# Front end and tail of a one-core H3 convolution and MLP kernel: k at the head of its queue, identity products on TensorE, a gate behind its copy, and a new written-out order

## The chip, the cores and the metric

The kernel runs on one core of one Trainium2 chip. The metric is the device time of one execution in microseconds (us). It was run three times before the change; the median is 254.28 us. Five engines work side by side: PE (TensorE, matrix products), DVE (VectorE), ACT (ScalarE), POOL (GpSimd) and SP, which only issues transfers. Products land in PSUM and must be copied ("evacuated") to SBUF by ACT or DVE.

## The reference, cut to what matters

```python
def _A_ref(q, k, v, shift_k, ssm_k, ssm_D):        # B, S, D = 1, 2048, 512; 4 shift taps
    k_shift = sum over t of  k_pad[:, t:t+S, :] * shift_k[:, 3-t]
    kv = k_shift * v
    y = irfft(rfft(kv, 2S) * rfft(ssm_k, 2S))[:S] + kv * ssm_D     # a long causal convolution
    return q * y
def _B_ref(x, w1, b1, w2, b2):                     # F = 1376
    return gelu(layernorm(x) @ w1 + b1) @ w2 + b2

x = A_q
x = x + _A_ref(layernorm(x), A_k, A_v, A_shift_k, A_ssm_k, A_ssm_D)
x = x + _B_ref(layernorm(x), B_w1, B_b1, B_w2, B_b2)
x = x + _A_ref(layernorm(x), ...)                  # the same k, v and filters again
x = x + _B_ref(layernorm(x), ...)
return x
```

The convolution's result y does not depend on x, so it is computed once and used twice.

## The kernel before, in words

There are two stages. The first, up to about 110 us, computes y by a transform written as matrix products, and starts on the first MLP. Its work is cut into pieces that are added to a `_Plan`; the order of the pieces, the engine that does each and the buffers that each takes stand in one long string, `ORDER`, written out by hand or by a search outside the kernel. `plan.write` emits the pieces in that order, so each engine works through its own pieces strictly in the order of the string. A word such as `kT3.P2` says: piece kT3, on PE, PSUM buffer 2 (there are four, of 1024 f32 each); `kT3e.A` says that its evacuation is done by ACT (D for DVE, G for POOL, S for a transfer issued by SP).

The pieces, in the order in which the data flow (lines of the kernel before):

- `lSK`, `lk0` to `lk3`, `lv0`, `lv1`, `lx0`, `lh…`, `lK..`: loads of the shift weights' row (into `SKr`, L164), of k (four transfers of 512 KB), v, the first group of x, edge rows of k, and the long filter (issued at L279 and L352). All stand on SP's one queue.
- `Dz` (L193): POOL spreads ssm_D, which a transfer from ACT's queue puts at byte 80 K of one large tile, the arena.
- `bS`, `bSK` (L364, L415): the shift weights turned into columns and broadcast by products with one row; `dg0` to `dg2` (L423) build diagonal matrices from them.
- `kT0` to `kT3` (L431): PE transposes of a quarter of k each, 12 per piece; evacuated at L217 (DVE) or L215 (ACT).
- `kv..` (L513): the shifted k as 32 products with the diagonals per piece; `kvm` (L519) multiplies with v on DVE. For the fourth column block POOL does the same by itself (`kg`, `ka`, `kgm`, L445 to L456). `s00` is the first layer norm's statistics.
- `U.S.` (L303), `KS` (L390), `U.T.` (L335, or by DMA transposes for the last column block, L282): first transform stage of kv and of the filter. `K2` (L403): second stage of the filter. `sa`, `sb`: eight SBUF to SBUF transfers of its result.
- `X` (L543), `T` (L558, DVE), `V` (L567): second stage of kv, product with the filter, first inverse stage; per column block 4 of each.
- `Z` (DMA transposes, L614) and `TC`, `TD` (PE transposes, L602); `Y` (L634): last inverse stage; `Y..e` copies Y into SBUF.
- per unit of rows of the first group, 0, 1 and 2 to 3: the gate `g0` (L660, L661: times normalised x, added to x), statistics `h0` (L237 to L243), POOL's power `p0` (L249), normalisation `b0` (L254), transposes `LT` (L642), and the first MLP product with GELU, `M` (L689, L697).

The second stage is a loop over eight groups of rows with products L726 (w1) and L760 (w2).

The gate reads the PSUM buffer of Y00 or Y01 itself, where `Y00e` and `Y01e` read the same buffer to copy it. The order before puts g00 ahead of Y00e, and Y01e ahead of g01.

Of the kernel before, what the change touches and what calls it, by code (L numbers as in the profile page):

```python
# [104 lines left out]
def kernel(ctx: ExitStack, tc: tile.TileContext, A_q, A_k, A_v, A_shift_k, A_ssm_k, A_ssm_D,  # L105
                 B_x, B_w1, B_b1, B_w2, B_b2, out):
    nc = tc.nc
    P = 128
    _, S, D = A_q.shape
    F = B_w1.shape[1]  # L110
    KS = A_shift_k.shape[1]
# [101 lines left out]
    def evac(eng, dst, src):  # L213
        if eng == "A":
            nc.scalar.activation(dst, src, AF.Copy)  # L215
        else:
            nc.vector.tensor_copy(dst, src)  # L217
# [56 lines left out]
    with tc.tile_pool(name="ps", bufs=1, space=bass.MemoryType.PSUM) as ps:  # L274
# [3 lines left out]
        def load(name, dst, src, nbytes, deps=(), eng="S", rank=0):  # L278
            return plan.add(name, {eng: 400}, deps, lambda it: nc.sync.dma_start(dst, src), dma=("copy", nbytes), rank=rank)  # L279
# [147 lines left out]
        for q in range(4):  # L427
            def mms(o, q=q):
                for i in range(4):
                    for ct in range(CK):  # L430
                        nc.tensor.transpose(o[:, i, ct, :], kn[:, 4 * q + i, ct * P:ct * P + P], IDt[:])  # L431
# [214 lines left out]
        for n, (a, b) in enumerate(UNITS):  # L646
            xs, ln, m = x_t[:, a:b, :], lna0[:, a:b, :], b - a
            if m == 1:
                y = plan.add(f"Y0{a}", {"P": 432}, e0[n] + [lH], lambda it, a=a: last_mm(0, a, 1)(
                    view(pf[it["slot"]["ps"]], [1, D])), take=["ps"])  # L650
                yf = [(y, "ps")]
                plan.add(f"Y0{a}e", {"A": 520, "D": 600}, [y], lambda it, y=y, a=a: evac(
                    it["eng"], YA[0][:, a:a + 1, :], view(pf[y["slot"]["ps"]], [1, D])), free=yf, rank=1)
            else:
                _, y = mm_evac("Y02", 864, e0[1] + [lH], last_mm(0, 2), [2, D], lambda: YA[0][:, 2:4, :])
                yf = []

            def gate(it, m=m, y=y, xs=xs, ln=ln, a=a, b=b):
                ya = YA[0][:, a:b, :] if m == 2 else view(pf[y["slot"]["ps"]], [1, D])
                nc.vector.tensor_tensor(ln, ln, ya, ALU.mult)  # L660
# [180 lines left out]
```

## Time and profile before

| | us |
|---|---|
| three runs | 257.37, 254.15, 254.28 |
| median | 254.28 |
| the profiled execution | 257.37 |
| its span, first to last instruction | 255.7 |
| granted TensorE clock, mean | 0.991 |
| PE, DVE, ACT, POOL busy | 237.9, 168.9, 145.6, 54.6 |
| first `kv` product starts | 15.57 |
| first product of `M` starts | 93.79 |
| loop's first product (L760) starts | 109.58 |

The profile shows one execution. "The chain of waits" follows the end of the program back to its start: each row has a start, a length and what was done there. "The timeline" lists the instructions of one engine; what stands in square brackets is the idle time before and what ended it. "The table by windows" gives busy time of each engine in a stretch of time, the number of instructions, the granted clock, and the DMA engines' share and rate.

### The profile page before, as it was taken

To read this page: it belongs to the slowest core of one execution; us is meant where nothing else is said; L and a number is where in the kernel's file an instruction comes from. 1 tells how busy PE (TensorE), PEld (TensorE's weight loads), DVE (VectorE), ACT (ScalarE), POOL (GpSimd) and SP (SyncE) were. 2 spreads that over 40 slices of the span, in tenths; PEclk is the share of its full clock that TensorE was granted. 3 is DMA by queue.
4 is the path that set the end of the run, shared out by engine and by line. 5 is a ranking of instruction groups with operands and counts; after the bars stand their busy time and mean duration, and the time that the engine had idled before them with its cause. 6 is when DMAs were issued, how large, how long until landed. Compare 5 with 4: busy or idle time off the path is not lost.

```text
span 255.7 us, 4760 instructions
## 1 busy us (share of the span) xinstructions
PE 237.9 (93%) x1907; PEld 150.5 (59%) x1919; DVE 168.9 (66%) x312; ACT 145.6 (57%) x221; POOL 54.6 (21%) x50
## 2 busy tenths in 40 slices
PE   1599999999999959999999999999999999999994
PEld 1489887799898748844444444444444444444443
DVE  0137789879999875787889899876866862022022
ACT  3677789999999667951722712812812812713700
POOL 4089999700000030111111101110110110000000
PEclk9999999999999988999999999999999999999999
DMA  2999997593959894013040402104006006001001
GB/s 72 313 309 226 198 363 299 242 387 123 288 119 159 212 243 160 3 23 62 0 85 0 82 0 55 30 0 82 1 22 146 0 21 146 1 26 57 3 33 49
DMA packets 51104, 29.65 MB, mean 116 GB/s; under 512 B 44707, under 2 KB 48520, under 8 KB 49802
## 3 DMA queue, kind: packets, MB, share of 16 engines
q1 hardware_dynamic: 50930, 29.21, 42.9%
q8 instruction: 15, 0.25, 0.4%
q10 hardware_dynamic: 152, 0.14, 0.2%
q14 instruction: 7, 0.06, 0.1%
HBM read 16.23 MB, written 2.10 MB: 72 GB/s over the span
## 4 chain that ended last, share of the span: by engine, by line
PE 78%; DMA 8%; ACT 5%; DVE 5%; issue 1%; SPq 1%; POOL 0%; ACTq 0%
PE po L760 30%; PE ph L726 26%; PE p L689 5%; PE p L513 4%; DMA arena<-ZT 4%; ACT arena L215 4%; DMA arena<-in_A_k_dram 3%; PE p L335 2%; PE p L543 2%; PE p L403 2%; ACT ZT L215 2%; PE p L303 1%; PE p L567 1%; PE p L634 1%; PE p L602 1%
## 5 line engine op out<-in xcount | busy, mean ns | idle before, releaser
L728 ACT ACTIVATE arena<-ph,B 128x512 bf16<-128x512 f32 (+1 forms) x77 | 52.7, 687 | 78.9 <-PE ph L726 78.9
L760 PE MATMUL po<-arena 128*128 128x512 bf16 (+3 forms) x355 | 77.0, 372 | 0.4
L726 PE MATMUL ph<-arena 128*128 128x512 bf16 (+1 forms) x308 | 67.6, 379 | 0.0
L760 PEld LDWEIGHTS <-arena 128*128 128x128 bf16 (+1 forms) x363 | 35.4, 98 | 40.7
L726 PEld LDWEIGHTS <-arena 128*128 128x128 bf16 (+1 forms) x308 | 30.8, 100 | 35.9
L765 DVE TENSOR_TENSOR arena<-po,arena 128x512 bf16<-128x512 f32 (+1 forms) x33 | 21.5, 672 | 44.3 <-PE po L760 44.3
L215 ACT ACTIVATE arena<-p 128x1024 bf16<-128x1024 f32 (+7 forms) x41 | 38.2, 1020 | 8.1 <-DVE arena L660 2.1
L249 POOL TENSOR_TENSOR lrsm<-lrsm,mhalf 128x4 f32<-128x4 f32 (+2 forms) x10 | 9.3, 926 | 94.0 <-DVE lrsm L243 94.0
L217 DVE COPY arena<-p 128x2048 bf16<-128x2048 bf16 (+4 forms) x13 | 12.9, 996 | 20.0 <-PE p L431 13.3
L215 ACT ACTIVATE ZT<-p 128x1024 bf16<-128x1024 f32 (+1 forms) x23 | 22.7, 1025 | 2.9 <-PE p L303 2.9
L237 DVE BATCH_NORM_STATS2 lstm<-arena 128x6 f32<-128x512 bf16 x32 | 20.0, 681 | 0.2
L558 DVE TENSOR_TENSOR T<-xb,arena 128x2048 bf16<-128x2048 bf16 (+1 forms) x17 | 18.9, 1152 | 0.0
L249 POOL TENSOR_TENSOR lrsg<-lrsg,mhalf 128x4 f32<-128x4 f32 x8 | 8.1, 1010 | 47.5 <-DVE lrsg L246 47.5
L237 DVE BATCH_NORM_STATS2 lstg<-arena 128x6 f32<-128x512 bf16 x28 | 17.2, 679 | 0.0
L445 POOL TENSOR_TENSOR T<-arena,SK 128x2048 bf16<-128x2048 bf16 (+3 forms) x4 | 14.9, 3744 | 9.3 <-ACT arena L215 9.1
L567 PE MATMUL p<-arena,T 128*128 128x128 bf16 x256 | 16.2, 219 | 0.8 <-ACT ZT L215 0.6
L254 DVE TENSOR_SCALAR arena<-arena,lmvg,lrsg 128x512 bf16<-128x512 bf16 x32 | 11.1, 409 | 7.9 <-POOL lrsg L249 7.9
L567 PEld LDWEIGHTS <-T 128*128 128x128 bf16 x256 | 15.0, 98 | 1.4 <-issue 0.8
L217 DVE CAST arena<-p 128x1024 bf16<-128x1024 f32 x13 | 15.3, 1219 | 0.7 <-PE p L390 0.6
L215 ACT ACTIVATE xb<-p 128x1024 bf16<-128x1024 f32 x14 | 14.4, 1048 | 0.1
L689 PE MATMUL p<-arena 128*128 128x128 bf16 (+3 forms) x132 | 11.8, 260 | 2.3 <-ACT arena L215 2.3
L513 PE MATMUL p<-DG,arena 128*128 128x128 bf16 x192 | 13.2, 235 | 0.0
(78 smaller groups left out, 250.4 us busy)
## 6 DMA issues: line engine op xcount, KB each, us to landing
arena<-arena SPq DMA_DIRECT2D x8, 512.0 KB, 5.3
arena<-in_A_k_dram SPq DMA_DIRECT2D x4, 512.0 KB, 6.2
arena<-in_A_v_dram SPq DMA_DIRECT2D x2, 1024.0 KB, 9.5
arena<-in_A_ssm_k_dram SPq DMA_DIRECT2D x4, 512.0 KB, 10.2
arena<-tabM SPq DMA_DIRECT2D x1, 2048.0 KB, 10.4
out_dram<-arena SPq DMA_DIRECT2D x15, 128.0 KB, 1.7
arena<-in_A_q_dram SPq DMA_DIRECT2D x1, 1536.0 KB, 7.7
arena<-in_B_w_dram SPq DMA_DIRECT2D x1, 1376.0 KB, 7.1
```

The costliest lines, as they stand in the source:

```text
L215: nc.scalar.activation(dst, src, AF.Copy)
L217: nc.vector.tensor_copy(dst, src)
L237: nc.vector.bn_stats(self.st[:, i, 0, :], x_t[:, GT * g + i, :] if src is None else src[:, i, :])
L249: nc.gpsimd.tensor_tensor(self.rs[:, a:b], self.rs[:, a:b], mhalf[:, a:b], ALU.pow)
L513: nc.tensor.matmul(o[:, i, :], w, DG[:, cc, t, :], start=t == 0, stop=t == KS - 1)
L558: eng.tensor_tensor(view(Tb[it["slot"]["T"]], [2, n, CW]), x2, kk, ALU.mult)
L567: nc.tensor.matmul(o[:, i, :], T[:, r, i, :], Mt[:, ka + i, 1 - r, :], start=r == 0, stop=r == 1)
L689: nc.tensor.matmul(o[0:m, ft - f0, :].rearrange("p (i t) -> p i t", t=P), W1t[:, ct, ft * P:ft * P + m], lnT[0][:, a:b, ct, :], start=ct = ...
L726: nc.tensor.matmul(o.rearrange("p (i t) -> p i t", t=P), W1t[:, ct, ft * P:ft * P + m], lt[:, a:b, ct, :], start=ct == 0, stop=ct == CT - 1)
L728: nc.scalar.activation(hT[0:m, ft, a * P:b * P], o, AF.Gelu_apprx_tanh, bias=B1[0:m, ft:ft + 1])
L760: nc.tensor.matmul(po[:, a:b], hT[0:m, ft, i * P:(i + 1) * P], W2t[0:m, ft, a:b], start=ft == 0, stop=ft == FT - 1)
L765: nc.vector.tensor_tensor(xs, po[:, a:b], xs, ALU.add)
```

## The change

Five edits, of which the last moves nearly every piece of the first stage:

1. `SKr`, the shift weights' row, moves from byte 80 K to 81 K of the arena, off the bytes into which ssm_D is loaded; `junk`, a scratch output of `s00`, moves from 84 K to 80 K.
2. k comes in two transfers of 1 MB instead of four of 512 KB (`lk1`: quarters 2 and 3, `lk0`: quarters 0 and 1).
3. Three new pieces `wm0` to `wm2`: 32, 4 and 4 products of the identity with itself, whose output nobody reads.
4. The gate of units 0 and 1 depends on the copy `Y0.e`, so that a written order must put the copy first.
5. A new `ORDER`.

```diff
-    SKr = at(80 * K, [[1, D * KS]], 0, 1)
+    SKr = at(81 * K, [[1, D * KS]], 0, 1)
...
-    junk = place("junk", [P, D], 84 * K)
+    junk = place("junk", [P, D], 80 * K)
...
-        lk = [load(f"lk{q}", kn[:, 4 * q:4 * q + 4, :], kd4[:, 4 * q:4 * q + 4, :], 2 ** 19) for q in range(4)]
+        lk = [load(f"lk{q}", kn[:, 8 * q:8 * q + 8, :], kd4[:, 8 * q:8 * q + 8, :], 2 ** 20) for q in range(2)]
...
+        def warm(it):
+            o = view(pf[it["slot"]["ps"]], [8, P])
+            for i in range(it["n"]):
+                nc.tensor.matmul(o[:, i % 8, :], IDt[:], IDt[:], start=True, stop=True)
+        for i, n in enumerate((32, 4, 4)):
+            it = plan.add(f"wm{i}", {"P": 107 * n}, [], warm, take=["ps"])
+            it["n"] = n
+            it["free"] = [(it, "ps")]
...
-                plan.add(f"Y0{a}e", {"A": 520, "D": 600}, [y], lambda it, y=y, a=a: evac(
+                ye = plan.add(f"Y0{a}e", {"A": 520, "D": 600}, [y], lambda it, y=y, a=a: evac(
...
-            ga = plan.add(f"g0{a}", {"D": 1190 if m == 2 else 930}, [y, s2, lx], gate, free=yf)
+            ga = plan.add(f"g0{a}", {"D": 1190 if m == 2 else 930}, [y, ye, s2, lx], gate, free=yf)
...
-lSK.S bSK.P0 bSKe.A bS.P2 lk3.S lk1.S lk0.S lk2.S lh113.S bSe.A ...
+lk1.S wm1.P0 wm0.P1 lSK.S wm2.P0 bS.P0 bSe.D dg1.D lk0.S dg0.A lh113.S bSK.P1 bSKe.A ...
```

What it moves, at three places. First SP's queue at the start of the program (k is `in_A_k_dram`, the shift weights' row `in_A_shift_k_dram`, the long filter `in_A_ssm_k_dram`); before:

```order
L279 DMA arena<-in_A_shift_k_dram 1x2048 [waits DMAHW1_49,Pool_49]
L279 DMA arena<-in_A_k_dram 128x2048 x4
L279 DMA kh<-in_A_k_dram 15x3x128
L279 DMA kh<-in_A_k_dram 112x3x128 [waits DMAHW0_49]
L279 DMA arena<-in_B_b_dram 1x1376
L279 DMA arena<-in_A_q_dram 128x2048 [waits DMAHW2_49]
L279 DMA arena<-in_A_v_dram 128x4096 [waits DMAHW3_49]
L352 DMA arena<-in_A_ssm_k_dram 128x32x64 [waits DMAHW4_49]
```

and after the change:

```order
L279 DMA arena<-in_A_k_dram 128x4096
L279 DMA arena<-in_A_shift_k_dram 1x2048
L279 DMA arena<-in_A_k_dram 128x4096
L279 DMA kh<-in_A_k_dram 15x3x128
L279 DMA kh<-in_A_k_dram 112x3x128
L279 DMA arena<-in_B_b_dram 1x1376
L279 DMA arena<-in_A_q_dram 128x2048 [waits DMAHW0_49]
L279 DMA arena<-in_A_v_dram 128x4096 [waits DMAHW1_49]
```

The first load of the queue no longer waits for POOL and for the load of ssm_D, k stands ahead of the shift weights, and both loads of v stand ahead of the long filter.

Second, DVE from the last inverse stage to the start of the MLP (L660 and L661 are the gate, L669 and L670 after the change; `lstm`, `lmvm`, `lrsm` are the statistics of a unit); before:

```order
L660 TENSOR_TENSOR arena<-arena,p_120 128x512
L661 TENSOR_TENSOR arena<-arena 128x512
L237 BN_STATS lstm_108<-arena 128x6
L241 BN_AGGR lmvm_109<-lstm_108 128x2
L243 TENSOR_SCALAR lrsm_110<-lmvm_109 128x1
L660 TENSOR_TENSOR arena<-arena 128x1024
L661 TENSOR_TENSOR arena<-arena 128x1024
L254 TENSOR_SCALAR arena<-arena,lmvm_109,lrsm_110 128x512
L237 BN_STATS lstm_108<-arena 128x6 x2
```

and after the change, where row 0's unit comes first and its copy out of PSUM (`L217 CAST`) is DVE's own:

```order
L217 CAST arena<-p_117 128x512
L669 TENSOR_TENSOR arena<-arena,p_117 128x512
L670 TENSOR_TENSOR arena<-arena 128x512
L237 BN_STATS lstm_108<-arena 128x6
L241 BN_AGGR lmvm_109<-lstm_108 128x2
L243 TENSOR_SCALAR lrsm_110<-lmvm_109 128x1
L669 TENSOR_TENSOR arena<-arena,p_120 128x512
L670 TENSOR_TENSOR arena<-arena 128x512
L254 TENSOR_SCALAR arena<-arena,lmvm_109,lrsm_110 128x512
```

The units now run in the order 0, 1, 2 to 3 (before: 1, 2 to 3, 0), and the gate of a two-row unit no longer stands between the first unit's statistics and its normalisation.

Third, ACT at the same place; before (the row that waits for DVE alone is the copy Y00e, and the 512-wide row behind it LT1e):

```order
L215 ACTIVATE arena<-p_118 128x1024 [waits DVE_49,PE_49]
L215 ACTIVATE arena<-p_119 128x512 [waits DVE_49]
L215 ACTIVATE arena<-p_117 128x512 [waits PE_49]
L215 ACTIVATE arena<-p_120 128x8x256
L215 ACTIVATE arena<-p_118 128x1024 [waits PE_49]
```

and after the change (the first 512-wide row is Y01e, the second LT0e):

```order
L215 ACTIVATE arena<-p_120 128x512 [waits PE_49]
L215 ACTIVATE arena<-p_119 128x1024
L215 ACTIVATE arena<-p_118 128x8x256 [waits PE_49]
L215 ACTIVATE arena<-p_120 128x512 [waits DVE_49,PE_49]
L215 ACTIVATE arena<-p_119 128x1024
```

Y00e has left ACT; the copy of the first transposed unit, LT0e, waits for DVE only because the PSUM buffer that its transposes took was read by the gate g01.

More of the change, by code (lines that the diff above doesn't have):

```diff
@@ L18 @@
 ORDER = """
-lSK.S bSK.P0 bSKe.A bS.P2 lk3.S lk1.S lk0.S lk2.S lh113.S bSe.A dg2.A dg0.A dg1.A lh1.S kg0.G kT3.P2 kT1.P0 kT1e.A kT3e.D kT0.P1 lb1.S kT0e.D kT2.P2 lx0.S lv0.S bB.P0 lK00.S lK01.S lv1.S kT2e.D kv20.P1 bBe.D lK11.S lK10.S kv00.P0 s00.A kvm20.D U2S0.P20 kvm00.D kv10.P1 U2S0e.D U2S1.P0 U2S1e.A U0S0.P31 U0S1.P2 kvm10.D U1S0.P12 U1S0e.D kv01.P0 U0S1e.A U0S0e.A kg1.G kd0.P1 U1S1.P2 kvm01.D kv11.P3 kvm11.D s01.G U1S1e.A kd0e.A KS11.P2 KS11e.A KS01.P1 KS01e.A KS30.P0 U0S2.P3 U0S2e.A KS30e.D KS00.P2 KS20.P1 KS21.P0 KS00e.D KS10.P3 KS20e.A KS10e.D kv21.P2 kd4.P3 KS21e.A U1S2.P0 kvm21.D kd4e.A U1S2e.A KS31.P1 KS31e.A lH.S KS51.P3 KS61.P2 KS51e.D KS61e.A KS41.P0 KS41e.D KS71.P1 KS50.P3 KS60.P2 KS71e.A KS50e.D KS40.P0 KS60e.A KS70.P1 lX.S KS70e.A KS40e.D U1S3.P3 U2S3.P2 U2S3e.D lW.S K22.P0 U1S3e.A K20.P1 K20e.D K23.P3 K25.P2 K22e.A K23e.A K25e.D K212.P0 K26.P1 K212e.A K21.P3 K26e.A lM.S K215.P2 K21e.D K210.P0 K27.P1 K210e.D K215e.A sa0.S K27e.A K29.P3 K24.P2 K24e.A U2S2.P0 K213.P1 K213e.A K29e.D sb0.S ka1.G kg2.G ka2.G kg3.G ka3.G K28.P3 K28e.A U2S2e.D U1T0.P2 K211.P0 sb1.S sa1.S K211e.A K214.P1 K214e.A U1T0e.D U2T0.P3 U0S3.P0 sa2.S sb3.S kgm.G U0S3e.A X10.P20 U2T0e.D U1T1.P1 X10e.A U1T1e.D X21.P31 U3S0.P02 U2T1.P2 U3S1.P1 X21e.A T10.D0 U3S0e.A U3S1e.A X20.P32 U0T0.P0 U2T1e.D X20e.A sb2.S sa3.S U3S3.P1 U3S3e.A X12.P20 T21.D1 X12e.A U0T0e.D U0T1.P3 X11.P11 U3S2.P0 T20.D2 U0T1e.D V10.P21 X11e.A U3S2e.A lx.S V10e.A U3T0.S ly.S U3T1.S V20.P10 X22.P32 T11.D0 T12.D2 X22e.A V21.P0 T22.D1 V21e.A X23.P21 X23e.A V20e.A X01.P30 V11.P0 V11e.A X01e.D V12.P2 X00.P32 X00e.A T23.D0 T01.D2 V22.P1 X13.P01 V12e.A T00.D1 X13e.A X03.P30 V23.P2 X03e.A V00.P0 V22e.D X02.P12 V23e.A T13.D0 T03.D1 V01.P3 X30.P21 X02e.A T02.D2 V01e.D V00e.A X30e.A V13.P1 V13e.A Z10.S Z11.S T30.D0 V03.P0 X32.P22 X31.P30 X31e.D X32e.A V03e.A V02.P1 T32.D2 V02e.A T31.D1 X33.P21 X33e.A TC0a.P0 V30.P32 V30e.A V32.P1 T33a.D0 V31.P2 T33b.D2 V33a.P3 TC0ae.D V32e.A V33ae.D Z03.S V33b.P1 TC0b.P0 Z00.S V31e.A V33be.A TD0a.P3 s02.D TC0be.A TD0ae.A TD0b.P2 TC1.P1 Z01.S TD0be.D Y01.P3 Y01e.A TC1e.D Y02.P2 g01.D h01.D TC3.P0 Y02e.A g02.D p01.G Y10.P1 TC3e.A w4.S b01.D Y00.P2 Y10e.A h02.D g00.D TC2.P3 Y00e.A w1.S LT1.P0 p02.G b02.D LT1e.A Y12.P1 h00.D TC2e.A M1a.P0 M1b.P2 LT2.P3 w3.S Z12.S Z13.S p00.G Z02.S Y12e.A M1be.A LT2e.D Y32.P1 M1ae.A M2a.P2 Y32e.A b00.D LT0.P3 M2b.P0 LT0e.A M2ae.A M2be.A M0a.P3 M2c.P2 M0ae.A M0b.P0 M0be.A M2ce.A Y20.P1 Y20e.A LG1.D Y22.P3 Y22e.A w2.S Y30.P0 Y30e.A
@@ new lines @@
+lk1.S wm1.P0 wm0.P1 lSK.S wm2.P0 bS.P0 bSe.D dg1.D lk0.S dg0.A lh113.S bSK.P1 bSKe.A lh1.S dg2.D kT3.P2 kT2.P0 kT2e.D kT3e.A lb1.S lx0.S lv0.S kT0.P1 lv1.S kT1.P3 kT0e.A bB.P2 bBe.A kT1e.D kv00.P1 kvm00.D kv10.P3 U0S0.P10 kv01.P2 kvm10.D U1S0.P31 s00.A U0S0e.A kvm01.D kv20.P0 U1S0e.D U0S3.P2 U0S1.P1 kv21.P3 U0S3e.D lK01.S U0S1e.A kvm20.D kvm21.D lK00.S kd0.P1 U1S1.P2 U2S0.P02 kd0e.A KS20.P1 U1S1e.A KS20e.D U2S0e.A KS21.P3 KS21e.A KS11.P2 lK11.S lK10.S KS11e.D lH.S KS00.P0 KS00e.D lX.S KS01.P1 KS31.P3 KS31e.A KS01e.A kv11.P2 KS30.P3 kd4.P0 KS10.P1 kd4e.A kvm11.D KS10e.D lW.S KS30e.A KS40.P0 kg0.G KS60.P2 KS60e.D KS61.P3 KS40e.A KS41.P1 KS71.P0 KS61e.A KS41e.D KS70.P2 KS71e.A KS70e.A KS50.P3 KS50e.D KS51.P1 U0S2.P0 U1S2.P2 U0S2e.D U2S3.P3 KS51e.A K210.P1 K211.P0 K210e.D U1S2e.A U2S3e.A kg1.G K29.P2 K29e.A K211e.D K214.P3 K23.P1 K214e.A K27.P2 K23e.D K20.P0 K22.P3 K20e.D K27e.A lM.S U1S3.P1 K22e.A s01.G K21.P2 K21e.D K25.P0 K213.P3 K213e.D U1S3e.A K25e.A K215.P1 K215e.A sa0.S K28.P2 K26.P0 ka1.G kg2.G ka2.G kg3.G K26e.D ka3.G K212.P3 U1T0.P1 K212e.D K24.P0 K28e.A sb0.S U0T0.P2 U2S2.P3 K24e.A U2S2e.A U1T0e.D U1T1.P0 U0T0e.D X10.P10 U1T1e.D X00.P31 U2S1.P2 X10e.A kgm.G U2S1e.A X00e.D U3S0.P01 sa3.S U3S0e.A T10.D0 U3S3.P1 X01.P22 U0T1.P3 X01e.A sa1.S U3S1.P0 X13.P20 sb1.S T00.D1 sb3.S U3S3e.A U2T0.P1 U0T1e.D U3S1e.A X13e.A U3S2.P3 sb2.S U3S2e.A V00.P0 V00e.A T01.D2 V10.P20 U2T0e.D X20.P12 T13.D1 X02.P31 V10e.A sa2.S X02e.A V13.P0 lx.S X20e.D T20.D0 X12.P20 V01.P1 V13e.A X12e.A X03.P32 V01e.A X03e.A T02.D1 U2T1.P0 T12.D2 X11.P21 U2T1e.D V20.P12 V12.P3 T03.D0 X11e.A V20e.A T11.D2 V12e.A X21.P00 X23.P22 X23e.D X21e.A V02.P1 X22.P31 V03.P0 T21.D1 U3T0.S V02e.A X22e.A T23.D0 V11.P2 X30.P10 ly.S U3T1.S V03e.A X30e.A V21.P3 X32.P02 T22.D2 X31.P11 V11e.A T30.D1 X31e.D X32e.A V23.P2 T32.D0 V21e.A V23e.A V30.P01 Z00.S Z01.S X33.P10 X33e.A Z10.S V22.P3 V22e.A V30e.A T31.D1 V32.P2 Z11.S Z03.S T33a.D2 T33b.D0 V32e.D V31.P1 V33a.P3 V33b.P0 TC0b.P2 w3.S w1.S V33ae.D V31e.A TC0a.P1 V33be.A TC0ae.D s02.D TC0be.A TD0a.P0 TD0b.P3 TD0ae.A w4.S TC1.P1 Y00.P0 TD0be.A Y02.P2 TC1e.A Y00e.D g00.D h00.D Y01.P3 Y01e.A g01.D p00.G Y02e.A TC2.P1 TC2e.A b00.D TC3.P0 Y12.P2 h01.D p01.G LT0.P3 g02.D LT0e.A Y12e.A Y10.P1 Y10e.A M0a.P3 b01.D LT1.P2 Z02.S Z12.S Z13.S LT1e.A h02.D M0b.P1 M0ae.A TC3e.D M1a.P2 M0be.A M1b.P0 p02.G b02.D LT2.P3 M1be.A LT2e.A Y30.P1 Y22.P0 M2b.P3 Y30e.A M1ae.A M2be.A M2a.P1 M2ae.A w2.S M2c.P2 M2ce.A Y32.P3 Y32e.A Y22e.A Y20.P1 Y20e.A LG1.D
```

5 lines of the change are left out of this document (3 added, 2 removed).

## The prediction

> **What bounds the kernel now.** I read the page first, for the span, and then the chain of waits, because its rows say what each stretch waits for.
>
> ```profile
> span 255.7 us, 4760 instructions
> ```
>
> ```profile
> 0.80 0.35 ACTq L184
> ...
> 3.37 0.25 POOL Dz L193
> ...
> 3.63 0.35 SPq L279
> ...
> 5.41 8.28 DMA arena<-in_A_k_dram
> ...
> 13.73 1.46 PE p L431 x12
> 15.19 0.38 PE p L370 x11
> 15.57 5.35 PE p L513 x64
> ...
> 25.10 1.79 PE p L513 x32
> ...
> 82.61 0.60 ACT ZT L215
> ...
> 93.79 4.24 PE p L689 x44
> ...
> 109.58 8.43 PE po L760 x39
> ```
>
> Read from the top: ACT issues its first transfer at 0.80, but SP's queue stands until POOL has spread ssm_D (3.37 to 3.62), because the shift weights' row overwrites those bytes. So k's last quarter lands at 13.69, and TensorE's real work, the kv products, starts at 15.57. From 109.58 to the end the chain is TensorE without a gap, in a loop that the change leaves as it is: the 146.1 us from there to 255.7 stay. Everything is decided by how much earlier L760 starts. Between the two, the table by windows shows which engine is full:
>
> ```profile
> core 0: us, PE busy (x) PEld busy (x) DVE busy (x) ACT busy (x) POOL busy (x), PEclk, DMA share, GB/s
> 42.00:53.00 11.00, 10.88 (x167) 9.00 (x162) 9.22 (x9) 10.58 (x13) 7.44 (x2) 1.00 0.59 241
> 53.00:65.00 12.00, 11.83 (x189) 11.54 (x186) 11.32 (x11) 12.00 (x14) 0.00 (x0) 1.00 0.71 247
> 65.00:75.50 10.50, 9.95 (x169) 9.61 (x169) 10.50 (x10) 10.50 (x13) 0.00 (x0) 1.00 0.85 226
> ```
>
> PE is full from 42 to 53, ACT from 53 on, DVE with it from 65. There is no stall to take out of this stretch; it can only start earlier or hold fewer pieces. Two slow spells of TensorE stand in the same table (columns as above):
>
> ```profile
> 12.20:15.60 3.40, 3.18 (x38) 2.71 (x36) 1.33 (x2) 1.88 (x2) 1.75 (x1) 1.00 1.07 402
> 15.60:19.00 3.40, 3.40 (x34) 3.40 (x35) 0.66 (x2) 3.24 (x10) 3.40 (x2) 1.00 1.16 239
> 19.00:22.40 3.40, 3.40 (x59) 3.35 (x58) 2.69 (x3) 2.69 (x8) 3.32 (x3) 1.00 1.04 165
> 90.70:94.10 3.40, 1.13 (x13) 0.71 (x11) 3.33 (x10) 1.45 (x3) 0.70 (x1) 1.00 1.23 227
> 94.10:97.50 3.40, 3.40 (x36) 3.40 (x34) 0.56 (x3) 2.32 (x2) 1.07 (x2) 0.50 0.95 263
> ```
>
> From 94.1 to 97.5 the granted clock is 0.50, after a window in which PE worked a third of the time. The column reads 1.00 at the start, yet kv is slow there: 64 products took 5.35, while 32 later ones took 1.79, 56 ns each. With twice 56 ns for the slow ones, 32 of the 64 were slow, 3.6 us. The rows agree: 34 products in 15.60 to 19.00, 59 in the next 3.40.
>
> **The change part by part.** *The head of SP's queue.* With the row moved, the first load (now k) can go when SP is free, about 0.80 as on ACT, where k's first load started at 4.05: 3.25 earlier.
>
> ```profile
> arena<-in_A_k_dram SPq DMA_DIRECT2D x1, 512.0 KB, 4.1
> 10.75 2.76 PE L431 MATMUL p<-IDt,arena 128*128 128x128 bf16 x24 [1.09 <-DMA arena<-in_A_k_dram]
> 15.23 0.96 DVE L217 COPY arena<-p 128x1536 bf16<-128x1536 bf16 x1 [0.72 <-PE p L431]
> ```
>
> *k in two loads.* Four loads took 13.69 - 4.05 = 9.64 from first issue to last landing (the first alone 4.1). No row shows a 1 MB load of k. Below: 2.1 MB at the 402 GB/s of the row 12.20 to 15.60 is 5.2; the first load's 4.1 less 1.3 at that rate leaves 2.8 of start-up, so landing 8.8. Above: as before plus ACT's tables in the way, 11.7. Same bytes, same queue, so I take 9.6, landing at 10.4. But now a half is transposed behind the last landing, not a quarter: 24 transposes of 2.76 (before 1.46), and kT1's copy of 0.96 on DVE stands ahead of the first kv. 10.4 + 2.76 + 0.96 + 0.2 of handing over is 14.3 against 15.57: **-1.3**. Had k stayed in quarters, the same landing would have given -3.2.
>
> *Identity products.* The forty have their operand at about 2.0 and nothing else to do; at 56 to 112 ns they take 2.2 to 4.5, over by 6.5, before half of k can have landed. They cost nothing; if k came early they would delay transposes that wait for the second half anyway, by at most 0.5. What they bring is bounded by the slow spells: 32 kv products at 56 ns less, 1.8, and about 1.0 of the 2.76 above. I take 0: between them and kv lie some 7 us in which PE does transposes and waits, and row 12.20 to 15.60 shows that transposes filling 3.18 of 3.40 did not speed it up.
>
> [...]
>
> *The middle.* The new order moves pieces but adds no work.
>
> ```profile
> 41.33 0.27 PE L403 MATMUL p<-arena,Wt 64*128 64x256 bf16 x1 [0.19 <-ACT arena L215]
> 52.62 0.61 PE L543 MATMUL p<-arena,Wt 128*128 128x128 bf16 x8
> 53.74 2.02 ACT L215 ACTIVATE xb<-p 128x1024 bf16<-128x1024 f32 x2
> 41.98 8.48 ACT L215 ACTIVATE arena<-p 128x1024 bf16<-128x1024 f32 x9
> 71.38 3.48 DVE L558 TENSOR_TENSOR T<-xb,arena 128x2048 bf16<-128x2048 bf16 x3
> ```
>
> Until the first K2 (41.33) PE now has one U product piece fewer (0.44): 41.33 - 1.3 - 0.4 = 39.6. From there to the first X (52.62, 11.3 later) one more piece of transposes (1.0): 51.9. From the first X's copy on, ACT has 31 copies of 1024 in both orders; at 8.48 / 9 = 0.93 with the last instruction's tail off they take 28.8, and before they ran 53.74 to 82.6 without a gap. Now the first X's copy can start at 52.5, as its two predecessors on ACT are done. That ends at 81.3, and V33be, the half copy behind them (82.61, 0.60), at 82.0 where it was 83.2: **-1.2**. DVE has 22 pieces of 1.13 from its first product T on, 25 us of the 27 to there: hidden under ACT. Bounds: 0, if U3T1 (below) lands when it did, to -2.0, if PE's piece fewer counts in full.
>
> *The tail.* The chain from V33be to the first M product took 93.79 - 83.2 = 10.6.
>
> ```profile
> 86.48 0.69 DVE L660 TENSOR_TENSOR arena<-arena,p 128x512 bf16<-128x512 bf16 x1 [0.17 <-ACT arena L215]
> 87.66 0.69 DVE L237 BATCH_NORM_STATS2 lstm<-arena 128x6 f32<-128x512 bf16 x1
> 88.68 0.68 DVE L660 TENSOR_TENSOR arena<-arena 128x1024 bf16<-128x1024 bf16 x1
> 88.84 0.96 POOL L249 TENSOR_TENSOR lrsm<-lrsm,mhalf 128x1 f32<-128x1 f32 x1 [39.32 <-DVE lrsm L243]
> 90.01 0.41 DVE L254 TENSOR_SCALAR arena<-arena,lmvm,lrsm 128x512 bf16<-128x512 bf16 x1
> 92.65 3.77 ACT L215 ACTIVATE arena<-p 128x512 bf16<-128x512 f32 x4 [2.13 <-DVE arena L660]
> ```
>
> The last row is the copy Y00e: ACT stood 2.13 for the gate g00 on DVE, with LT1e, which M waits for, queued behind. Now: TD0a, TD0b and TC1 on PE 1.7, Y00 0.45, its copy on DVE 0.7, gate 1.15 (86.48 to 87.66), statistics 1.05 (to 88.68). While POOL takes the power (0.96), DVE does unit 1's gate, 1.15; then normalisation 0.4, LT0 0.3, its copy 0.55, handing over 0.4: 7.8. The first M starts at 89.8: **-2.8** more. Y01's gate now waits for ACT's copy, done while DVE is at unit 0. Bounds: -4 (TC1 not in the way) to 0 (a late DMA transpose Z, or w1, decides).
>
> *M.* 132 products and the Y's between them took 109.58 - 93.79 = 15.8, of which 44 took 4.24 for 2.46 at 56 ns: 1.8 of slow clock. PE now has Y12, LT0 and Y10 (2.0 in all) in the 2.3 before the first M, so the slow spell is less likely; I keep 0.5 of 1.8: **-1.3**, bounds -1.8 to 0.
>
> *Sum.* -1.2 (start and middle), -2.8, -1.3: -5.3. [...] I add 0.6 for that: **-4.7**. The profiled span would be 251.0. The profiled execution took 257.37, 3.1 above the median, 1.7 of it outside the span; I carry the difference over to the median: 254.28 - 4.7 = **249.6**.
>
> **The rivals.** *A: the clock stays fast into kv.* For it: forty products and an earlier kv. Against: row 12.20 to 15.60. It gives 1.8 and some of the 1.0 more, 2.4: 247.2.
>
> *B: the middle gives the start back.* The fourth column block goes through two DMA transposes in a queue behind eight copies and a load of x.
>
> ```profile
> 64.85 0.54 SPq L279
> ...
> 65.44 9.98 DMA arena<-ZT
> ...
> 75.47 1.19 PE p L543 x16
> ```
>
> Landing at 75.42, it held X32 up by a moment. My walk has its input 2.2 earlier, but sa and sb now wait for K2 pieces further apart. If it lands when it did, the 1.2 is lost, and with 0.6 of the tail's bounds used: 251.4.
>
> [...]
>
> *D: the change doesn't do what it says:* the load of k starts no earlier, for a wait that the queue's rows don't show. Then kv starts 2.0 late and the sum is -1.4: 252.9.
>
> **How the numbers follow.** Forecast 0.51, A 0.14, B 0.26, C 0.04, D 0.05. The forecast's own range is 247.6 to 251.6. Two in ten left out: 246.8 to 252.6, which holds most of A, all of B, and the bounds of k's landing. A measurement of this kernel tells about 2% (5.1 us) from no change. Below 249.2 lie two fifths of the forecast, A and a little of B and nothing else: faster 0.40. Above 259.4 lies the tail of C: 0.02. Same: 0.58.
>
> **What would show it.** In the changed kernel: k's first issue near 0.8; kv (L521) near 14.3, at 107 to 112 ns for its first 3.4 us or more; kT near 115 ns each; first K2 near 39.6; V33be done near 82; ACT no longer held by the gate; the first M near 89.8; L760 near 104.9. It is wrong if kv is fast from its first product, if PE waits at X32 or inside M, or if the loop (L735) waits for its transposed rows, which now have about 1 us to spare.

## The result and the profile after

| | before | after |
|---|---|---|
| median of 20 runs each, side by side | 255.80 | 253.45 |
| the profiled execution | 257.37 | 254.56 |
| its span | 255.7 | 252.8 |
| granted TensorE clock, mean | 0.991 | 0.993 |

The ratio of the means is 0.9925 (that of the medians 0.9908), with a 95% interval of 0.9897 to 0.9953: 1.9 us less, where 4.7 less was forecast. It lies within 2% of no change. Of all runs below, one is left out of the figures: an execution of the last kernel of the experiments took 351.55, at a mean granted clock of 0.664. In the profiled executions, the loop's first product comes 3.1 us earlier and the span is 2.9 shorter.

The chain of waits of the kernel after (start, length, what was done), with the stretch that matters in full:

```profile
7.45 3.92 PE p L439 x36
...
12.90 3.75 PE p L521 x64
...
56.94 1.03 ACT arena L215
57.97 0.02 issue
57.98 0.47 SPq L279
...
58.56 0.53 SPq L279
59.09 0.05 issue
59.14 5.69 SPq L282
...
64.93 0.52 SPq L279
65.44 0.05 issue
65.50 9.60 DMA arena<-ZT
75.10 0.05 issue
75.14 1.11 PE p L551 x16
...
83.79 0.64 ACT ZT L215
...
92.36 1.79 PE p L698 x32
...
106.48 9.67 PE po L769 x44
```

The start is better than forecast: 64 kv products take 3.75, where they took 5.35. But between 58 and 75 no engine computes on the chain. It runs through SP's queue: ACT's copy V00e ends at 57.97, and only then SP issues sa2 (57.98, the last of the eight SBUF to SBUF transfers), lx (58.56), the transpose U3T0 (59.14), ly (64.93) and U3T1 (65.50), whose data X32 on PE waits for. In the kernel before, the same transpose was issued long after the copies, in 1.97:

```profile
55.20 1.03 SPq L279 DMA_DIRECT2D arena<-in_A_q_dram  x1
62.32 1.97 SPq L282 DMA_TRANSPOSE arena<-ZT  x1
```

Three views of the kernel after show what the late sa2 holds up. SP's waits in total, times and longest; then one row each of DVE, ACT and PE:

```profile
SPq L279 <- ACT arena L215: 7.2, 3, 6.5
```

```profile
62.53 2.36 DVE L566 TENSOR_TENSOR T<-xb,arena 128x2048 bf16<-128x2048 bf16 x2 [1.77 <-DMA arena<-arena]
```

```profile
62.52 1.02 ACT L215 ACTIVATE arena<-p 128x1024 bf16<-128x1024 f32 x1 [0.89 <-DMA arena<-arena]
```

```profile
75.14 1.11 PE L551 MATMUL p<-arena,Wt 128*128 128x128 bf16 x16 [3.27 <-DMA arena<-ZT]
```

SP stood 6.5 us for that one copy. When sa2 at last landed, T02 on DVE had waited 1.77 and V01e on ACT 0.89; X32 then waited 3.27, where it had waited 0.3 before. The table by windows (columns as in the prediction's) shows one thing more:

```profile
72.00:76.00 4.00, 0.86 (x16) 0.86 (x17) 1.97 (x2) 1.16 (x3) 0.00 (x0) 1.00 0.87 178
76.00:78.00 2.00, 2.00 (x23) 2.00 (x21) 1.22 (x1) 1.74 (x3) 0.00 (x0) 0.51 1.03 198
78.00:80.00 2.00, 2.00 (x26) 2.00 (x25) 1.56 (x2) 1.02 (x1) 0.00 (x0) 0.64 1.00 187
```

After four microseconds in which PE worked 0.86, the granted clock is 0.51: the 32 products behind X32 take 3.37 (105 ns each) instead of some 1.8. ACT, which the prediction took to be full from the first X's copy on, stands at both places:

```profile
49.59 1.02 ACT L215 ACTIVATE xb<-p 128x1024 bf16<-128x1024 f32 x1 [0.44 <-PE p L551]
...
75.80 1.02 ACT L215 ACTIVATE xb<-p 128x1024 bf16<-128x1024 f32 x1 [2.84 <-PE p L551]
...
80.16 1.02 ACT L215 ACTIVATE xb<-p 128x1024 bf16<-128x1024 f32 x1 [1.14 <-PE p L551]
```

The first row is the copy of the first X; the bracket of the second is the wait at X32, that of the third the slow products. Below, the clock is called closed where 0.50 is granted and open where 1.00 is. At the start of the program the column reads 1.00 throughout (0 to 40 in the kernel after), while products of the same 128x128 form take 110 to 118 ns each there at some times and 56 to 63 ns at others. The first is near the 105 ns measured at 0.51 to 0.64 above, the second near the 56 ns of 32 products at 1.00 (60.77 in the kernel before, 1.79). For the start, closed and open are the author's reading of the time of a product, an estimate from these two; the column does not show it.

Cut in four, the account closes. The marks are DVE's first product with v (kvm, L519 and L527), the end of V33be's copy, the first M product and the loop's first product (L760 and L769).

| us | before | after | difference |
|---|---|---|---|
| to the first kvm | 19.14 | 14.96 | -4.2 |
| kvm to V33be's copy done | 64.1 | 69.5 | +5.4 |
| V33be to the first M product | 10.6 | 7.9 | -2.7 |
| M to the loop's first product | 15.8 | 14.1 | -1.7 |

### The profile page after: what moved, and what is told of

Its sections match the earlier page's. It is cut to its first block, busy times and chain, and to the rows that moved or that the text cites. A ratio compares the mean times of both kernels' runs of the same rounds, so it can differ in the third digit from the quotient of the medians.

```text
span 252.8 us, 4848 instructions
## 1 busy us (share of the span) xinstructions
PE 240.5 (95%) x1959; PEld 152.5 (60%) x1959; DVE 172.5 (68%) x321; ACT 143.0 (57%) x212; POOL 54.8 (22%) x50
## 4 chain that ended last, share of the span: by engine, by line
PE 76%; ACT 13%; DMA 4%; SPq 3%; DVE 2%; issue 1%; POOL 0%; ACTq 0%; DVEq 0%; POOLq 0%
PE po L769 30%; PE ph L735 26%; ACT arena L215 5%; DMA arena<-ZT 4%; ACT arena L706 4%; PE p L521 4%; ACT ZT L215 4%; PE p L403 3%; SPq L282 2%; PE p L335 2%; PE p L420 2%; PE p L575 2%; PE p L610 2%; PE p L439 2%; PE p L303 1%
## 5 line engine op out<-in xcount | busy, mean ns | idle before, releaser
L769 PE MATMUL po<-arena 128*128 128x512 bf16 (+2 forms) x363 | 77.4, 372 | 0.1
L769 PEld LDWEIGHTS <-arena 128*128 128x128 bf16 (+1 forms) x363 | 35.5, 98 | 40.9 <-issue 0.3
L215 ACT ACTIVATE arena<-p 128x1024 bf16<-128x1024 f32 (+8 forms) x41 | 38.8, 1025 | 6.0 <-PE p L383 1.3
L215 ACT ACTIVATE ZT<-p 128x1024 bf16<-128x1024 f32 (+1 forms) x24 | 23.5, 1022 | 2.5 <-PE p L303 2.2
L217 DVE CAST arena<-p 128x1024 bf16<-128x1024 f32 (+1 forms) x16 | 18.2, 1185 | 1.6 <-PE p L642 0.7
L575 PE MATMUL p<-arena,T 128*128 128x128 bf16 x256 | 17.7, 231 | 1.2 <-ACT arena L215 0.8
L575 PEld LDWEIGHTS <-T 128*128 128x128 bf16 x256 | 16.4, 104 | 1.7 <-issue 1.2
L215 ACT ACTIVATE xb<-p 128x1024 bf16<-128x1024 f32 x12 | 12.3, 1035 | 4.5 <-PE p L551 4.4
L254 DVE TENSOR_SCALAR arena<-arena,lmvm,lrsm 128x512 bf16<-128x512 bf16 x32 | 11.3, 410 | 2.2 <-POOL lrsm L249 2.2
L217 DVE COPY arena<-p 128x2048 bf16<-128x2048 bf16 (+2 forms) x10 | 10.7, 1074 | 2.8 <-PE p L439 2.4
L551 PE MATMUL p<-arena,Wt 128*128 128x128 bf16 x128 | 9.2, 219 | 3.4 <-DMA arena<-ZT 3.3
```

The source lines that it names most:

```text
L254: nc.vector.tensor_scalar(out=dst[:, i, :], in0=xs, scalar1=self.mv[:, i, 0:1], scalar2=self.rs[:, i:i + 1], op0=ALU.subtract, op1=ALU.mult)
L575: nc.tensor.matmul(o[:, i, :], T[:, r, i, :], Mt[:, ka + i, 1 - r, :], start=r == 0, stop=r == 1)
L769: nc.tensor.matmul(po[:, a:b], hT[0:m, ft, i * P:(i + 1) * P], W2t[0:m, ft, a:b], start=ft == 0, stop=ft == FT - 1)
```

## The experiments

Each median is of 6 runs (after: 20; row back: 12; the last kernel: 5) beside runs of the kernel before (median 255.8 to 256.2). The last column is the ratio's distance from 1 times 256. The two columns of starts are of one profiled execution each, by the chain of waits for the loop; that of "sa2 early" took 251.55, 1.4 above its median, that of "no products" 251.50, 2.3 below. The profile of the last kernel is of one further execution (249.84).

| kernel | first kvm | loop's first product | median | us against before (95%) |
|---|---|---|---|---|
| after | 14.96 | 106.5 | 253.45 | -1.9 (-2.6 to -1.2) |
| sa2 early | 16.73 | 103.4 | 250.14 | -6.0 (-7.0 to -5.1) |
| x late | 14.73 | 103.2 | 250.95 | -4.8 (-5.8 to -3.8) |
| no products | 15.24 | 103.4 | 253.75 | -3.1 (-4.1 to -2.1) |
| sa2 early, no products | 15.01 | 101.7 | 249.99 | -5.8 (-6.7 to -4.8) |
| sa2 early, quarters | 15.35 | 102.1 | 250.10 | -5.7 (-6.8 to -4.7) |
| sa2 early, neither | 14.88 | 101.9 | 249.85 | -6.0 (-7.3 to -4.8) |
| sa2 early, row back | 18.90 | 105.7 | 253.99 | -2.0 (-2.8 to -1.3) |
| sa2 early, gate first | 14.36 | 101.5 | 250.11 | -5.9 (-7.1 to -4.7) |
| before, row alone | 16.22 | 106.1 | 252.55 | -4.1 (-5.1 to -3.1) |
| before, copy first | 17.80 | 105.2 | 253.49 | -2.9 (-4.0 to -1.9) |
| before, row and copy | 15.00 | 102.1 | 249.89 | -5.7 (-6.8 to -4.6) |

**sa2 early.** In the built program sa2 waits for ACT's count up to V00e, though the bytes that the two write lie apart (80 to 88 K and 100 to 108 K of the arena); moved ahead of V00e in the order, it is free of that wait.

```diff
-... U3S2.P3 sb2.S U3S2e.A V00.P0 V00e.A ... V10e.A sa2.S X02e.A ...
+... U3S2.P3 sb2.S sa2.S U3S2e.A V00.P0 V00e.A ... V10e.A X02e.A ...
```

> The changed kernel with one word of its order moved: the copy sa2 stands right behind sb2, ahead of the piece V00e, so that it no longer waits for ACT's copy V00e (in the changed kernel it is issued at 57.98, after 6.5 us of SP's waiting). Theory 1 (the late sa2 holds up the two DMA transposes behind it, and through them X32 and the clock): sa2 goes before 54, U3T0's issue takes about 2 us instead of 5.7, U3T1 lands by 72 instead of 75.1, X32 does not wait (3.3 now), the clock stays at 1.00 from 76 to 80 (0.50 now), the loop's first product (L769) comes at 103 to 104 instead of 106.5, and the time is about 5 below the kernel before, where the changed kernel is 1.9 below it. Rival (the transposes' own transfers and the load ly between them set the landing): U3T1 still lands at 74.5 to 75.5, X32 waits 3, L769 at 106 to 106.5, time 1.5 to 2.3 below the kernel before.

SP's queue and the same windows, of this kernel:

```profile
48.29 6.02 SPq L279 DMA_DIRECT2D arena<-arena  x6
54.43 0.92 SPq L279 DMA_DIRECT2D arena<-in_A_q_dram  x1
58.61 2.24 SPq L282 DMA_TRANSPOSE arena<-ZT  x1
60.95 0.73 SPq L279 DMA_DIRECT2D arena<-in_A_q_dram  x1
61.73 6.70 SPq L282 DMA_TRANSPOSE arena<-ZT  x1
```

```profile
72.00:76.00 4.00, 3.69 (x65) 3.51 (x63) 4.00 (x5) 4.00 (x5) 0.00 (x0) 1.00 0.54 105
76.00:78.00 2.00, 2.00 (x40) 2.00 (x37) 2.00 (x2) 2.00 (x4) 0.00 (x0) 1.00 0.98 183
```

All copies are out by 54.3, U3T0 goes when its input is there (58.6), its issue takes 2.24, and PE runs through X32 at a granted clock of 1.00. One word of the order was worth 4 us. The rival falls.

**x late.** Which harm of the late sa2 costs more, its own landing or the queue behind it?

```diff
-... V13.P0 lx.S X20e.D ... X30.P10 ly.S U3T1.S ...
+... V13.P0 X20e.D ... X30.P10 U3T1.S lx.S ly.S ...
```

> The changed kernel with sa2 left where it is (behind V00e), but with the loads of x, lx and ly, moved behind the second DMA transpose: U3T0, U3T1, lx, ly. It parts the two harms of the late sa2. Theory 1a (what costs is the transposes' place behind sa2, lx and ly, and the full queue): U3T0 goes at 58.6, U3T1 lands at 70 to 72, X32 waits under 0.5, the clock stays at 1.00, and most of the gain of the run with sa2 early comes back: 4.5 to 5.5 below the kernel before. Theory 1b (what costs is sa2's own landing at 62.4, which T02 and V01e wait for, 2 us of PE's and ACT's time, and the full queue behind it): U3T0's issue still takes over 4, U3T1 lands at 73 or later, and the time is 2 to 3.5 below the kernel before. Rival (two transposes one behind the other slow each other): U3T1 at 75 as now, 1.9 below.

PE's rows where V01e and X32 are waited for:

```profile
64.33 1.05 PE L575 MATMUL p<-arena,T 128*128 128x128 bf16 x16 [1.84 <-ACT arena L215]
...
72.45 1.06 PE L551 MATMUL p<-arena,Wt 128*128 128x128 bf16 x16
```

sa2's landing still costs PE 1.84 at 64.3, but X32 starts at 72.45 without a wait, and most of the gain is there, as theory 1a has it. By the runs the queue is the larger part (about 2.9), the landing the smaller (about 1.2). The intervals overlap, and the edit also takes the 1.5 MB of ly from ahead of U3T1, where they stand in the kernel before too: U3T1 landed 4.3 after its issue here, and 9.6 in the kernel after. So the split is rough. U3T0, right behind sa2, took 4.4 to issue here, where it took 1.94 to 2.62 in six profiles in which the copies were out early (5.69 in the kernel after).

**No products, and sa2 early with no products.**

```diff
-lk1.S wm1.P0 wm0.P1 lSK.S wm2.P0 bS.P0 ...
+lk1.S lSK.S bS.P0 ...
```

> The changed kernel without the forty identity products. Theory 2 (the identity products opened the clock for the first kv products): kv's first 64 products take 5.0 to 5.4 again, as before the change (3.75 with them), the first K2 (L411) comes 1.5 to 1.8 later than 36.27; at the end little of it is left, since U3T1's landing at 75.1 decides, not the start: X32's wait shrinks from 3.3 to about 1.6 and the time is 1.0 to 2.0 below the kernel before. Rival (the 48 transposes in one stretch of 4.65 opened it, and the identity products did nothing): kv's 64 take 3.7 to 3.8 also without them, K2 at 36.3, and the time is as the changed kernel's, 1.9 below the kernel before.

> The changed kernel with sa2 early (behind sb2) and without the forty identity products, so that no wait in the middle hides what they do. Theory 2, now doubted (they open the clock for kv): kv's first 64 slow, 5.0 to 5.4, time 4.2 to 4.8 below the kernel before. Theory 2b (k's 48 transposes, which now run without a gap, open the clock; the products are worth nothing, and kvm waits for v anyway): kv's 64 take 3.75, L761's first product at 102.5 to 104, time 5.6 to 6.4 below the kernel before, as with them.

Both times no worth of the products can be measured: kv's 64 take 3.75 without them, and the rival of the first run and theory 2b of the second hold. PE's rows of the second kernel:

```profile
7.37 5.30 PE L431 MATMUL p<-IDt,arena 128*128 128x128 bf16 x48
12.60 0.42 PE L370 MATMUL p<-one,arena 1*128 1x1 bf16 x11
12.96 3.75 PE L513 MATMUL p<-DG,arena 128*128 128x128 bf16 x64
```

With 48 transposes ahead, all at 110 ns, and otherwise only some two dozen products with one row, kv is fast from its first product (59 ns). "No products" and "sa2 early, neither" have the 48 in one stretch too, of 4.17 and 4.87, and the same 3.75 behind it. So in these three profiles the transposes alone stood ahead of a fast kv, and the late wait at X32 is not what hid the products' worth. (Without them and with sa2 late the time is not told apart from the kernel after: -3.1 and -1.9, with intervals that overlap.) With the identity products, what they do differs from one execution to the next. The kernel after:

```profile
2.07 4.45 PE L420 MATMUL p<-IDt 128*128 128x128 bf16 x40 [2.07 <-POOL mhalf L189]
```

and the one with sa2 early and k in quarters:

```profile
2.07 3.92 PE L420 MATMUL p<-IDt 128*128 128x128 bf16 x40 [2.07 <-POOL mhalf L189]
...
7.13 1.51 PE L439 MATMUL p<-IDt,arena 128*128 128x128 bf16 x24
```

In the second k's transposes ran at 63 ns, an open clock by that time; in the kernel after the first 16 of them took 1.89, 118 ns each. "x late", which is the kernel after up to this place, has 3.95, and 1.51 for the first 24 transposes. It did not matter, for the next reason.

**sa2 early, quarters; sa2 early, neither.** k in four loads of 512 KB; the second also without the products.

```diff
-lk1.S wm1.P0 wm0.P1 lSK.S wm2.P0 bS.P0 bSe.D dg1.D lk0.S ...
+lk3.S lk2.S wm1.P0 wm0.P1 lSK.S wm2.P0 bS.P0 bSe.D dg1.D lk0.S lk1.S ...
```

> The changed kernel with sa2 early and k in four loads of 512 KB instead of two of 1 MB, at the same places of the queue (two ahead of the shift weights' row, two where lk0 stood). Theory 3 (the size of the load does nothing for the landing; being at the queue's head does): the last k lands at 8.5 to 9.5 as with two loads (8.8), kv starts at 12.8 or up to 0.5 earlier, and the time is 5.5 to 6.5 below the kernel before. Rival (1 MB loads are what made k land 1.6 earlier than my 10.4): the last quarter lands at 10 or later, kv starts at 13.5 to 14.5, time 4.5 to 5.3 below.

> The changed kernel with sa2 early, k in four loads of 512 KB and no identity products: of the five edits only the row, the gate behind its copy and the order are left. Theory 5 (neither the two loads nor the products do anything, alone or together): 5.6 to 6.4 below the kernel before, as with both of them (6.0) or with either. Rival (one stands in for the other, so that taking one away showed nothing): kv's first 64 take over 4.5, the time is 4.0 to 5.0 below.

With quarters k's last load lands at 10.2 (two loads: 8.8 to 9.3), so the landing is later, as the rival had it; but kv starts at 11.70 and 12.82, and the time is the same. Theory 5 holds. What decides the first kvm is the later of kv and v. DVE's first kvm with sa2 early, with both other edits in:

```profile
16.73 2.36 DVE L527 TENSOR_TENSOR arena<-p,arena 128x1024 bf16<-128x1024 f32 x2 [3.78 <-DMA arena<-in_A_v_dram]
```

and with sa2 early and no products:

```profile
15.01 1.23 DVE L519 TENSOR_TENSOR arena<-p,arena 128x1024 bf16<-128x1024 f32 x1 [1.35 <-PE p L513]
```

In the first kernel kv started at 12.83 and DVE then stood 3.78 for v; in the second kv started later, at 12.96, and kvm came earlier. Of the nine profiles with the new order, six have the first kvm behind v's landing and three (after, "sa2 early, no products", "sa2 early, neither") behind kv. From the first kvm to the loop's first product all six kernels with sa2 early take 86.7 to 87.2, whatever lies ahead of it.

**sa2 early, row back.**

```diff
-    SKr = at(81 * K, [[1, D * KS]], 0, 1)
+    SKr = at(80 * K, [[1, D * KS]], 0, 1)
...
-    junk = place("junk", [P, D], 80 * K)
+    junk = place("junk", [P, D], 84 * K)
```

> The changed kernel with sa2 early and with the first edit taken back: the shift weights' row at 80 K again, junk at 84 K. lk1 still heads the queue, but lSK waits for POOL's spreading of ssm_D, and lk0, v and x stand behind it. Theory 4 (the start of the queue is what the edit is worth, also in the new order): the load of v goes 2 to 3 later and lands after 17, the first product with v on DVE (L527) starts at 17.5 to 19 instead of 15 to 16.7, the first K2 (L411) at 38.5 to 40 instead of 36.3 to 37.8, and the time is 3.0 to 4.5 below the kernel before. Rival (with half of k at the queue's head the edit no longer matters): L527 at 15 to 16.7, time 5.5 to 6.4 below.

The row is worth 4.0 here, more than the 1.5 to 3 that theory 4 gives it. SP's queue:

```profile
0.80 0.41 SPq L279 DMA_DIRECT2D arena<-in_A_k_dram  x1
6.77 0.31 SPq L279 DMA_DIRECT2D arena<-in_A_shift_k_dram  x1
```

With 1 MB of k under way, the 4 KB of ssm_D take 5.05 to land, so the shift weights' load waits until 6.77 (3.63 in the kernel before), and v and kvm (18.90) with it.

**sa2 early, gate first.** Row 0's gate ahead of its copy again, the copy on ACT.

```diff
-... TC1e.A Y00e.D g00.D h00.D ...
+... TC1e.A g00.D Y00e.A h00.D ...
...
-            ga = plan.add(f"g0{a}", {"D": 1190 if m == 2 else 930}, [y, ye, s2, lx], gate, free=yf)
+            ga = plan.add(f"g0{a}", {"D": 1190 if m == 2 else 930}, [y, s2, lx], gate, free=yf)
```

> The changed kernel with sa2 early and the fourth edit taken back for row 0's unit: g00 ahead of the copy Y00e, Y00e on ACT, the gate not tied to it. Theory 6 (the copy behind the gate makes ACT stand, in the new order as in the old): ACT waits 1 to 2 at Y00e for g00 on DVE, with Y01e and Y02e queued behind it, so the second unit's gate, and M later on, come 1 to 2 later; time 4.0 to 5.2 below the kernel before. Rival (in the new order nothing urgent stands behind Y00e, and DVE is spared a copy of 0.7): first M product (L698) 0.3 to 0.7 earlier against V33be, time 5.8 to 6.8 below.

ACT, whose idle time is in brackets:

```profile
78.83 9.84 ACT L215 ACTIVATE arena<-p 128x768 bf16<-128x768 bf16 x11
```

Eleven copies without a gap: in the new order the gate is done by the time ACT reaches Y00e. The theory's wait is not there. M comes 8.3 behind V33be, where the other kernels with sa2 early have 7.8, so the rival's gain is not there either; the time is the same within the intervals. In the old order the place of the copy is worth more:

**Before, row alone; before, copy first; before, row and copy.** The first edit alone in the kernel before; the word Y00e.A ahead of g00.D alone; both.

```diff
-... h02.D g00.D TC2.P3 Y00e.A ...
+... h02.D Y00e.A g00.D TC2.P3 ...
```

> The kernel before with the first edit alone: the shift weights' row at byte 81 K, junk at 80 K; order, loads of k and all else as before. By the prediction's sum the queue starts at 0.8 instead of 4.05, k's last quarter lands at about 10.4, kv starts near 12.4 instead of 15.57 and all of it reaches the end: 3 below the kernel before. Theory (the start is given back in the middle): kv starts near 12.4, but ACT and DVE, full from 53 on, and the landing of U3T1 move by less than half of it, and the time is 0 to 1.5 below the kernel before.

> The kernel before with the copy Y00e ahead of the gate g00 in the order, and nothing else. By the prediction ACT's stall of 2.13 goes, LT1e and the first M product (L689) come about 2.1 earlier (91.7 instead of 93.79), the slow spell inside M stays, and the time is 1.7 to 2.3 below the kernel before. Rival (M's first product is held by DVE's or POOL's chain for unit 1 as well, so that the stall covered nothing): L689 at 93.3 or later, time 0 to 0.7 below.

> The kernel before with the row at 81 K and the copy Y00e ahead of g00, and nothing else of the change: no 1 MB loads, no identity products, the old order. If the two edits are worth their gains alone and these add up (3.6 and 2.7 below the kernel before), the time is 6.0 to 6.6 below, L760's first product at 102.5 to 103.5: then the new order, the two loads and the identity products bring nothing beside them. Rival (both shorten the same wait, or the middle caps the sum): 3.6 to 4.6 below, L760 at 104.5 to 106.

> A profile of the kernel before with the row at 81 K and the copy Y00e ahead of g00, which was timed at 5.8 below the kernel before. The row's edit alone brought L760's first product to 106.1, the copy's alone to 105.2, from 109.6. If both gains are there in full, it starts at 102 to 103.5, with the first product with v on DVE (L519) at 15 to 16.7 as in the other kernels with the row at 81 K, and the stretch from V33be's copy to the first M product (L689) at 7.5 to 8.5 (10.6 before).

The row alone moves the first kvm by 2.9, the loop's first product by 3.5 and the time by 4.1; the middle gives none of it back in the old order, against my theory. Three of its six executions show a mean granted clock of 0.998 or 1.00 and take 251.3 to 251.8, the other three 0.990 to 0.993 and 253.3 to 253.9; the profile is of the second kind, with M's first 44 products in 4.18. None of the 11 executions of the kernel before beside them is above 0.993. So part of the 4.1 is probably the clock, by the author's estimate from these mean clocks. The copy alone: ACT's and PE's rows,

```profile
85.63 7.54 ACT L215 ACTIVATE arena<-p 128x1024 bf16<-128x1024 f32 x7 [0.27 <-PE p L634]
```

```profile
90.55 2.62 PE L689 MATMUL p<-arena 128*128 128x128 bf16 x44
```

where ACT had a wait of 2.13 in the middle and the 44 products took 4.24. From V33be (82.4) to M it is 8.1 instead of 10.6, from M to the loop 14.7 by the chain (105.2) instead of 15.8; the first kvm is 1.3 earlier, as kv was faster in this execution (its 64 products took 4.36, where they took 5.35), and the middle takes 0.5 longer. With both edits the first M comes 8.4 behind V33be (78.7), as expected, M then waits 0.75 for a DMA transpose Z, and the loop starts at 102.1, where it was expected. Together the two small edits give 5.7 by the runs, less than the 7.0 of their sum by 1.3, which the intervals allow. That is as much as all five edits with sa2 mended, and the 87.1 from the first kvm to the loop are the same too: the new order, the 1 MB loads and the identity products add nothing that can be measured.

## Why the prediction was wrong, point by point

| step | forecast | measured |
|---|---|---|
| k's first issue | 0.8 | 0.80 |
| k's last landing | 10.4 (8.8 to 11.7) | 8.8 |
| kT, ns each | 115 | 97 |
| first kv product | 14.3 | 12.90 |
| kv's first 64 | slow, 5.3 | 3.75 |
| first K2 | 39.6 | 36.27 |
| V33be done | 82.0 | 84.43 |
| V33be to the first M | 7.8 | 7.9 |
| M to the loop | 14.5 (15.8 - 1.3) | 14.1 |
| L769, with the 0.6 added for kv's clock | 104.9 | 106.5 |

- **The step that failed is the middle**: "before they ran 53.74 to 82.6 without a gap. Now the first X's copy can start at 52.5 [...] That ends at 81.3". It took ACT to be full in the new order as in the old. The first X's copy started at 49.59, 2.9 before the forecast; yet those 31 copies ended at 83.8 instead of 81.3, as ACT stood 0.89 for sa2, 2.84 for X32 and 1.14 behind the slow products. From the first kvm to V33be the kernel after took 69.5, the kernel before 64.1. The new order put a wait into SP's queue that the rows of before could not show: sa2 behind V00e. The walk looked at what the transposes need (sa and sb "wait for K2 pieces further apart"), not at what each issue on SP waits for. Moving the one word gives 4 us back: this is shown.
- **Rival B named the place and not the price.** "If it lands when it did, the 1.2 is lost": U3T1 landed at 75.10, as before (75.42). But the work ahead of X32 had moved 3.3 us forward, so PE stood 3.27 and lost some 1.6 behind it, where the granted clock was 0.51 to 0.64 (3.37 for 32 products instead of 1.8); V33be came 1.2 later instead of at the same time.
- **The start was sized too small**: k landed at the lower bound, the transposes then ran without a gap, and kv's first 64 took 3.75, an open clock by their time. Rival A had that effect (chance 0.14) with the wrong cause; without the identity products it is the same 3.75. No run shows the 0.6 that the sum adds for kv's clock; kv's 64 took 3.75 in all nine profiles of the new order, 1.6 less than before. The reading of row 12.20 to 15.60, that transposes do not speed kv up, did not carry over to them. In the kernel before they stood in three pieces with gaps of 1.09 and 0.22 between them, and kv's 64 took 5.35; with the copy first the gaps are 0.81 and 0.16, and kv's took 4.36; with the row alone there is one gap, 0.85, ahead of 36 in one stretch, with row and copy they are 0.35 and 0.37, and kv's took 3.75 both times. That the gaps are what kept the clock closed is the author's estimate from these rows and was not tried by itself.
- **The tail and M were right**: -2.7 for -2.8 and -1.7 for -1.3, and the copy alone in the old order gave -2.5 and -1.1. But their cause in the kernel after is not only the fourth edit, since in the new order taking it back for unit 0 costs 0.5 in the profile and nothing that shows in the time. And M's path changed: in the kernel after the chain from 94.41 to 106.44 runs over ACT's copies and GELUs, so without the slow spell (the granted clock is 1.00 from 92 to 98), ACT and not PE sets M's length there.
- The sum of the measured parts with an untouched middle, -4.2 - 2.7 - 1.7, is -8.6 by the profiled executions. Three of the kernels with sa2 early reach -7.6 to -7.8 in span (248.1 and 247.9 against 255.7), and -6 by the medians, since the profiled execution of the kernel before lay 1.6 above its median. What is left, some 0.9, is 0.5 to 0.9 of the middle, which takes 64.6 to 65.0 in these three kernels against 64.1, and up to 0.3 of the loop, which takes 146.2 to 146.4 to the end against 146.1. Which engine holds the middle was not tried.
- **The base was low too.** The forecast's 249.6 stands on the 254.28 of three runs; 20 runs of the same kernel have 255.80. So 1.5 of the distance to 253.45 is the base and not the change. And the 1.7 outside the span was no part of the 3.1: the kernel after has 1.8 outside its span as well.

## What to carry to other kernels

When an order is rewritten, walk the issuing queue too: for each transfer, what it now waits for, and what stands behind it. A copy that is an engine's own business can hold up the whole first stage when a transfer waits for it with transposes queued behind: here SP stood 6.5 for one copy, and moving one word was worth about 4. A start gained on one load is worth only as much as the next load allows: here k landed 5 us earlier, and in six of nine profiles v, behind it, decided. And price the edits one at a time: in the old order one changed address and one moved word gave as much as all five edits once their order was mended.

## What the runs showed of the hardware

- The issue of the first DMA transpose (U3T0) took 1.94 to 2.62 us in six profiles in which the copies ahead of it had been issued over 3 us before (before, row alone, copy first, sa2 early, and sa2 early with no products or with quarters), and 3.96 to 5.69 in the three in which it came within 1.2 us of one (no products, x late, after). Why was not tried.
- A 4 KB load from another queue (ssm_D) took 1.9 to land in the kernel before and in the one with the copy first, where SP's queue stood still, and 4.8 to 5.5 where k's loads were issued at once; here with sa2 early:

```profile
1.20 5.04 DMA arena<-in_A_ssm_D_dram
```

- The mean granted clock differs between executions of one kernel. In the kernel after, 4 of 20 executions have 0.999 or 1.00 and take 252.9 on average; the other 16 have 0.987 to 0.993 and take 253.9. Without the identity products it is 1 of 6, the profiled one, in which X32 waited 2.58 and the clock stayed at 1.00; in the profile of the kernel after X32 waited 3.27 and it fell to 0.51. With sa2 early all 6 have 0.998 or 1.00.
